# Turning q and k of the second batch over on DVE in 32x32 squares instead of on PE

## The chip, the cores and the metric

The kernel runs on one core of a Trainium2 chip. The metric is the device time of one execution in microseconds (us), lower is better. The engines are PE (TensorE: matmuls and transposes, results go to PSUM), DVE (VectorE), ACT (ScalarE), POOL (GpSimd) and SP (SyncE, here only a queue that issues DMAs). All data is float32 on the chip; the two weight matrices arrive as float64 and are narrowed on the chip.

## The reference

Attention that keeps the 32 largest scores of each row, and behind it a two-layer perceptron with an exact GELU:

```python
# q, k, v: (8, 8, 576, 64); w_in: (512, 2048); w_out: (2048, 512)
scores = q @ k.transpose(0, 1, 3, 2) / sqrt(64)
kth = np.partition(scores, -32, axis=-1)[..., -32:-31]
scores = np.where(scores >= kth, scores, -1e9)
attn = softmax(scores)                       # exp(s - max) / (sum + 1e-9)
x = (attn @ v).transpose(0, 2, 1, 3).reshape(8 * 576, 512)
h = x @ w_in
out = (0.5 * h * (1 + erf(h / sqrt(2)))) @ w_out
```

## The kernel before

**Tiles.** The 8 heads of a batch are taken as 4 pairs, so there are 32 pairs; pair 4 to 7 are the second batch. A pair's 576 rows are four tiles of 128 rows (two heads at a time) and a rest of 64; the rests of two pairs make one more item. A batch has 18 items, and the kernel 144.

**The main loop.** It runs over slots n = 0 to 147 and writes out, in program order, the work of several items at different stages: DVE looks for the 32 largest of item n (`top_k`: MAX8 and MATCH_REPLACE8), PE makes the scores of item n + 2 (`scores`, L370 and L385), ACT applies the softmax of item n - 1 (L495, L496), POOL divides it by its sum (`normalise`, L507), PE turns over the probabilities of item n - 2 (`transposes`, L527 and L553) and multiplies those of item n - 3 with v (`attend`, L615), and ACT copies that product into `xT` (L620). From slot 11 on PE's remaining time is filled with pieces of the perceptron (`mlp`: L673 for the first layer, L755 and others for the second); before that, with dummy matmuls (`keep_busy`, L995). Each engine works its instructions off in this order. A slot closes on DVE with the reciprocal of the softmax's sums (`inverse`, L482), which waits for POOL's `den` (L488), which waits for ACT's exponentials.

**Keys and queries.** Scores need q and k with the head dimension on the partitions, so both are turned over, pair by pair, into `kt` (keys, and the rest rows of q) and `qm` (q). A pair has three pieces: c = 0 (four key tiles), c = 1 (the rests of k and q), c = 2 (four query tiles). There are two ways. `by_pe` (L281) has PE transpose the 128x128 tiles of `raw_k` and `raw_q` into a PSUM bank, `tp_qk`, from which ACT copies them (L286). `squares` (L268, L270, L272) has DVE transpose 32x32 blocks straight from `raw_k` and `raw_q` into `kt` and `qm`; for that `load` brings the data in with the blocks' places already exchanged, in 16 transfers a pair (L109), with rows of 128 bytes, instead of 8 transfers (L116, L119) with rows of 256 bytes. `SQUARES` is the first pair that goes by DVE. A pair below it has one of two raw buffers, by its parity (the second lies in an unused part of `w_sum`), and its loads are issued when the pair two before it has been read; a pair from `SQUARES` on has the one buffer, and its loads are issued when the pair just before it has been read.

**Where the pieces stand.** `slots_of` gives the slots of the pieces by PE, `squares_of` those by DVE, both counted from the first item of the batch (18 for the second batch). Pieces by DVE stand at the head of their slot, behind `larger` (L406); pieces by PE stand among the transposes of the slot.

**PSUM.** `bank` hands out four banks in turn up to slot 12 and from slot 13 on the one bank "z" (`few`), which `tp_qk`, `tp_t` and `o` share.

**Weights.** `w_in` and `w_out` come in 16 units of two 128x512 parts. `load_weights` (L188, on SP) is called at the end of the slot two before the one in which the unit is added up; ACT (L205, L206, L212) or DVE (L208) splits the words in the slot before, and POOL adds them (L227).

Of the kernel before, what the change touches and what calls it, by code (L numbers as in the profile page):

```python
# [14 lines left out]
def kernel(  # L15
# [30 lines left out]
    NP = H // 2  # L46
# [38 lines left out]


    n_pairs = B * NP
    SQUARES = 2 * NP
    sources = {"q": q, "k": k, "v": v}

    def raw_of(n, pair):
        if n != "v":
            return raws[n][pair % 2 if pair < SQUARES else 0]
        return raws[n][pair % len(raws[n])]

    def load(n, pair, queue=None, queue2=None):
        if pair >= n_pairs:
            return
        queue = queue or nc.sync
        queue2 = queue2 or queue  # L100
        b, h0 = pair // NP, 2 * (pair % NP)
        src = sources[n]
        if n != "v" and pair >= SQUARES:
            t = flat[n][0]
            for e in range(2):
                for d in range(2):
                    rows, cols = slice((2 * e + d) * SQ, (2 * e + d + 1) * SQ), slice(d * SQ, (d + 1) * SQ)
                    for at, lo, hi, by in ((0, 0, SM, queue), (SM + e * TL, SM, S, queue2)):
                        by.dma_start(  # L109
                            out=t[rows, at : at + hi - lo].rearrange("i (c j) -> i c j", j=SQ),  # L110
                            in_=src[b, h0 + e, lo:hi, cols].rearrange("(c i) j -> i c j", i=SQ),
                        )
            return
        t = raw_of(n, pair)
        for e in range(2):
            queue.dma_start(  # L116
                out=t[:, 0:NM, e, :], in_=src[b, h0 + e, 0:SM].rearrange("(t p) d -> p t d", p=P)
            )
            queue2.dma_start(out=t[e * TL : (e + 1) * TL, NM, e, :], in_=src[b, h0 + e, SM:S])  # L119
# [140 lines left out]
    def transpose_qk(pair, first=False):  # L260

        q_tail = SM + P
        done = set()

        def squares(c):
            rq, rk, kt = flat["q"][0], flat["k"][0], kt_of.get(pair)
            if c == 0:
                nc.vector.transpose(kt[:, 0:q_tail], rk)  # L268
            elif c == 1:
                nc.vector.transpose(kt[:, q_tail:], rq[:, SM:])  # L270
            else:
                nc.vector.transpose(q_of[pair], rq[:, 0:SM])  # L272

        def by_pe(c):
            rq, rk = raw_of("q", pair), raw_of("k", pair)
            group = (
                [(rk, j) for j in range(NM)], [(rk, NM), (rq, NM)], [(rq, j) for j in range(NM)]
            )[c]
            tp = bank("tp_qk")
            for x, (r, j) in enumerate(group):  # L280
                nc.tensor.transpose(  # L281
                    tp[:, x * P : (x + 1) * P], r[:, j].rearrange("p e d -> p (e d)"), ident
                )
            dst = (kt_of[pair][:, 0:SM], kt_of[pair][:, SM:], q_of.get(pair))[c]
            copy = nc.vector.tensor_copy if first and c < 2 else nc.scalar.copy
            copy(out=dst, in_=tp[:, 0 : len(group) * P])  # L286

        def piece(c):
            if c == 0:
                kt_of[pair] = work.tile([P, 2 * P + SM], f32, tag="kt", bufs=NP + 2, name="kt")  # L290
            if c == 2:
                q_of[pair] = work.tile([P, SM], f32, tag="qm", bufs=NP, name="qm")
            (squares if pair >= SQUARES else by_pe)(c)
            done.add(c)
            ahead = 1 if pair >= SQUARES else 2
            if pair + ahead > SQUARES and pair < SQUARES and pair % 2:
                return
            if c != 0 and done >= {1, 2}:
                load("q", pair + ahead)
            if (c == 0 if pair >= SQUARES else c != 0 and done >= {0, 1, 2}):  # L300
                load("k", pair + ahead)

        return [lambda c=c: piece(c) for c in range(3)]
# [694 lines left out]
    for pair in range(2):  # L998
# [12 lines left out]
    squares_of = [  # L1011
# [4 lines left out]
    ]  # L1016
    first = {2: (0, 1, 1), 3: (2, 2, 3)}
    prep_in, squares_in = {}, {}
    for pair in range(2, n_pairs):
        b, p = divmod(pair, NP)  # L1020
        if pair >= SQUARES:
            trio = transpose_qk(pair)
            for at, c in squares_of[b % 2 * NP + p]:
                squares_in.setdefault(starts[b] + at, []).append(trio[c])
            continue
        for at, piece in zip(first.get(pair, slots_of[b % 2][p]), transpose_qk(pair)):
            prep_in.setdefault(starts[b] + at, []).append(lambda _, piece=piece: piece())
# [140 lines left out]
```

## Time and profile before

| | |
|---|---|
| runs | 1553.4, 1556.66, 1557.61 us; median 1556.66 |
| profiled execution | 1557.3 us, its span 1555.5 us, granted PE clock 0.994 |
| busy in the span | PE 98%, DVE 86%, ACT 75%, POOL 73% |
| DMA | 56.35 MB in 185298 packets, 176161 of them under 512 bytes |

The span runs from the first to the last instruction of the program; the execution's own time has 1.8 us more around it. An engine's busy time is the time in which at least one of its instructions runs; matmuls overlap, and their ends are modelled. In a group of instructions the last column is the time that the engine stood idle just ahead of them, with the instruction of another engine that ended it. A name as `L281` is a line of the kernel, and a `q` behind an engine's name its queue.

### The profile page before, as it was taken

How to read it: one execution, taken by the hardware profiler on the slowest of the kernel's cores; microseconds unless marked ns; L12 is line 12 of the kernel's file. 1: busy time of each engine (PE TensorE's matmuls, PEld its weight loads, DVE VectorE, ACT ScalarE, POOL GpSimd, SP SyncE). 2: the span in 40 equal slices, each digit the busy share in tenths (PEclk: the TensorE clock that was granted, in tenths of full speed). 3: DMA queues.
4: the chain of work that ended last, by engine and by line, in shares of the span. 5: the costliest groups of instructions: out<-in, count | busy, mean ns of one | idle time of the engine just before them, and what ended most of it. 6: DMA issues, size and time to landing. Idle time of an engine off the chain costs nothing. (4 is left out here: it accounts for less than half of the span.)

```text
span 1555.5 us, 28139 instructions
## 1 busy us (share of the span) xinstructions
PE 1522.8 (98%) x9280; PEld 1199.5 (77%) x9280; DVE 1330.3 (86%) x4571; ACT 1165.3 (75%) x2050; POOL 1141.5 (73%) x1291
## 2 busy tenths in 40 slices
PE   7899999999999999999999999999999999999998
PEld 5676578877777778887777778787877777787887
DVE  8998799989999988998989997988998998988700
ACT  6998877767777777777777778777777777777720
POOL 4886567767787868777787877776788786877632
PEclk9999999999999999999999999999999999999999
DMA  6513210012101111012201111002110111000000
GB/s 180 158 61 117 89 45 1 1 37 54 24 15 31 35 26 31 1 30 42 39 18 16 30 31 45 1 23 36 34 24 22 24 30 32 15 1 15 7 14 14
DMA packets 185298, 56.35 MB, mean 36 GB/s; under 512 B 176161, under 2 KB 176705, under 8 KB 185153
## 3 DMA queue, kind: packets, MB, share of 16 engines
q1 hardware_dynamic: 183888, 54.13, 14.6%
q8 instruction: 73, 1.20, 0.3%
q14 instruction: 73, 0.59, 0.1%
q10 hardware_dynamic: 1200, 0.39, 0.1%
q0 software_dynamic: 64, 0.03, 0.0%
HBM read 45.08 MB, written 9.44 MB: 35 GB/s over the span
## 5 line engine op out<-in xcount | busy, mean ns | idle before, releaser
L673 PE MATMUL h_ps<-xT,w_in_sb 128*128 128x256 f32 (+1 forms) x2560 | 541.4, 362 | 1.9 <-ACT xT L620 1.9
L673 PEld LDWEIGHTS h_ps<-xT,w_in_sb 128*128 128x128 f32 x2560 | 435.4, 191 | 73.4 <-issue 25.3
L450 DVE MAX8 top<-lists 128x8 f32<-128x288 f32 x792 | 321.1, 447 | 0.0
L507 POOL TENSOR_TENSOR s<-s,rden 128x1152 f32<-128x1152 f32 x144 | 302.7, 2102 | 0.3 <-DVE rden L482 0.3
L496 ACT ACTIVATE s<-s,bias 128x576 f32<-128x576 f32 x288 | 223.3, 775 | 11.9
L453 DVE MATCH_REPLACE8 lists<-top,lists 128x288 f32<-128x288 f32 x528 | 229.8, 443 | 0.0
L495 ACT ACTIVATE s<-s,neg 128x576 f32<-128x576 f32 x288 | 225.7, 784 | 2.8 <-POOL neg L475 2.7
L450 DVE MAX8 low<-lists 128x8 f32<-128x288 f32 x528 | 213.1, 445 | 0.0
L574 ACT COPY pt<-tp 128x1024 f32<-128x1024 f32 x133 | 134.8, 1014 | 96.1 <-PE tp L553 96.1
L488 POOL TENSOR_SCALAR den<-den 128x2 f32<-128x2 f32 x144 | 31.4, 218 | 236.0 <-ACT s L496 232.1
L421 POOL TENSOR_TENSOR lists<-lists 128x576 int32<-128x576 int32 x132 | 186.3, 1411 | 4.0
L413 POOL TENSOR_TENSOR lists<-s 128x576 int32<-128x576 int32 x132 | 185.6, 1406 | 0.0
L553 PE MATMUL tp<-ident,s 128*128 128x128 f32 x1152 | 150.7, 274 | 7.7 <-POOL s L507 7.7
L553 PEld LDWEIGHTS tp<-ident,s 128*128 128x128 f32 x1152 | 133.7, 141 | 27.3 <-POOL s L507 14.0
L615 PE MATMUL o<-pt,raw_v 128*64 128x256 f32 x1280 | 154.1, 386 | 0.4 <-ACT pt L560 0.4
L615 PEld LDWEIGHTS o<-pt,raw_v 128*64 128x64 f32 x1280 | 86.9, 137 | 87.0 <-issue 44.7
L475 POOL TENSOR_SCALAR neg<-kth 128x2 f32<-128x2 f32 x132 | 85.6, 649 | 88.3 <-DVE kth L466 88.3
L482 DVE RECIPROCAL rden<-den 128x2 f32<-128x2 f32 x144 | 23.4, 162 | 139.8 <-POOL den L488 138.6
L811 PE MATMUL y_ps<-w_out_sb,sum 128*128 128x256 f32 x480 | 142.8, 379 | 0.0
L378 ACT ACTIVATE s<-s_ps 128x1024 f32<-128x1024 f32 x127 | 124.3, 1025 | 15.7 <-PE s_ps L370 15.5
L370 PE MATMUL s_ps<-kt,qm 64*128 64x512 f32 x512 | 131.2, 626 | 0.8 <-ACT s L376 0.8
L453 DVE MATCH_REPLACE8 lists<-low,lists 128x288 f32<-128x288 f32 x264 | 114.9, 443 | 0.0
(148 smaller groups left out, 2784.1 us busy)
## 6 DMA issues: line engine op xcount, KB each, us to landing
raw_v<-in_v_dram SPq DMA_DIRECT2D x64, 128.0 KB, 2.4
out_dram<-y SPq DMA_DIRECT2D x30, 256.0 KB, 2.1
w_out_sb<-in_moe_w_in_dram SPq DMA_DIRECT2D x14, 511.8 KB, 4.9
raw_q<-in_q_dram SPq DMA_DIRECT2D x96, 64.0 KB, 2.0
raw_k<-in_k_dram SPq DMA_DIRECT2D x96, 64.0 KB, 2.0
w_out_sb<-in_moe_w_out_dram SPq DMA_DIRECT2D x10, 511.8 KB, 4.1
w_sum<-in_moe_w_out_dram SPq DMA_DIRECT2D x6, 511.8 KB, 4.1
raw_q<-in_q_dram SPq DMA_DIRECT2D x96, 8.0 KB, 1.8
```

The source lines that it names most:

```text
L413: nc.gpsimd.tensor_tensor(t[:, 1].bitcast(i32), a.bitcast(i32), b.bitcast(i32), op=ALU.add)
L421: nc.gpsimd.tensor_tensor(both, both, top, op=ALU.subtract)
L450: nc.vector.max(x[:, e], src[:, e])
L453: nc.vector.match_replace(dst[:, e], x[:, e], src[:, e], LOWEST)
L495: nc.scalar.activation(s, s, func=AF.Prelu, bias=st["neg"][:, e : e + 1], scale=1.0, alpha=STEEP)
L496: nc.scalar.activation(s, s, func=AF.Exp, bias=st["bias"][:, e : e + 1], scale=1.0, accum_out=st["den"][:, e : e + 1],)
L507: nc.gpsimd.tensor_tensor(s, s, wide, op=ALU.mult)
L553: nc.tensor.transpose(tp[:, j * P : (j + 1) * P], s[:, first + j * P : first + (j + 1) * P], ident)
L574: nc.scalar.copy(out=pt_now[0][:, 0 : 2 * NM, x : x + P], in_=tp.rearrange("p e (j n) -> p (e j) n", j=NM),)
L615: nc.tensor.matmul(o[e * D : (e + 1) * D, 0:n], lhsT=vt[:, j, e, :], rhs=pt[:, e * NM + j if j < NM else 2 * NM, :], start=(j == 0), stop= ...
L673: nc.tensor.matmul(h_tile(u)[:, i, :], lhsT=w_in_sb[:, ko, f * P : (f + 1) * P], rhs=xT[:, ko, c0 : c0 + n], start=(ko == 0), stop=(ko == ...
L811: nc.tensor.matmul(acc[names][:, k], lhsT=lhsT, rhs=rhs, start=(j == 0 and k == 0), stop=(j == FT // 2 - 1 and k == 1),)
```

## The change

`SQUARES` falls from 8 to 4, so that pairs 4 to 7 go by DVE too. A list of its own, `second`, gives their pieces' slots: 12 to 17. Pairs 0 to 3 stay with PE.

```diff
-    SQUARES = 2 * NP
+    SQUARES = NP
...
+    second = [
+        [(-6, 0), (-5, 1), (-5, 2)], [(-5, 0), (-4, 1), (-4, 2)],
+        [(-3, 0), (-3, 1), (-3, 2)], [(-2, 0), (-2, 1), (-1, 2)],
+    ]
...
         if pair >= SQUARES:
             trio = transpose_qk(pair)
-            for at, c in squares_of[b % 2 * NP + p]:
+            for at, c in second[p] if b == 1 else squares_of[b % 2 * NP + p]:
                 squares_in.setdefault(starts[b] + at, []).append(trio[c])
             continue
```

The pieces of pairs 4 to 7 stood in slots 8 to 10, 11 to 13, 14 and 15, and 15 and 16. In the new program the 40 transposes L281 and 12 copies L286 of these pairs are gone, twelve DVE transposes stand in slots 12 to 17, and the loads of pairs 4 to 7 are 64 transfers instead of 32: pair 4's are issued in slot 1, where they stood before, pair 5's in slots 12 and 13, pair 6's in 13 and 14, pair 7's in 15. The order of all else on PE, ACT, DVE and POOL is as before.

## The prediction

> **What bounds the kernel now.** A *slot* is one pass of the kernel's main loop; I cut the trace where DVE's reciprocal (L482) starts, which happens once in a slot. Read first is the page's list of engines: it names PE, but as an average over stages.
>
> ```profile
> PE 1522.8 (98%) x9280; PEld 1199.5 (77%) x9280; DVE 1330.3 (86%) x4571; ACT 1165.3 (75%) x2050; POOL 1141.5 (73%) x1291
> ```
>
> The stage is therefore read by itself, in the view of stretches: slots 11 to 17, from one reciprocal to the next. A row gives stretch, length, busy time and count of PE, PEld, DVE, ACT, POOL, then PE's granted clock, DMA share and GB/s.
>
> ```profile
> 112.33:123.90 11.57, 11.33 (x55) 8.13 (x53) 8.85 (x32) 7.43 (x15) 5.87 (x6) 0.90 0.48 127
> 123.90:133.29 9.39, 9.18 (x55) 7.30 (x56) 8.86 (x33) 9.25 (x17) 5.87 (x6) 1.00 0.34 132
> 133.29:145.98 12.69, 12.46 (x51) 5.99 (x49) 9.45 (x34) 12.52 (x20) 8.62 (x7) 1.00 0.08 18
> 145.98:157.43 11.45, 10.77 (x75) 8.30 (x71) 9.46 (x34) 8.74 (x16) 8.62 (x7) 1.00 0.64 213
> 157.43:169.65 12.22, 11.47 (x55) 5.78 (x53) 9.45 (x33) 12.05 (x18) 8.62 (x7) 1.00 0.09 16
> 169.65:182.07 12.42, 11.96 (x80) 8.38 (x79) 9.46 (x34) 9.12 (x16) 8.62 (x7) 1.00 0.46 121
> 182.07:194.08 12.01, 12.01 (x54) 5.79 (x54) 8.78 (x32) 11.44 (x17) 5.38 (x5) 1.00 0.25 89
> ```
>
> PE fills nearly all of each row, ACT fills every second one, and DVE has 2.6 to 3.3 us over in all but slot 12. The groups of this stretch (busy us and mean ns, then idle time before and its releaser) say who waits for whom.
>
> ```profile
> L553 PE MATMUL tp<-ident,s 128*128 128x128 f32 x56 | 7.4, 273 | 0.0
> ...
> L281 PE MATMUL tp_qk<-ident,w_sum 128*128 128x128 f32 x20 | 3.3, 281 | 1.4 <-ACT qm L286 0.7 <-ACT kt L286 0.5 <-ACT pt L537 0.2
> L281 PE MATMUL tp_qk<-ident,raw_q 128*128 128x128 f32 x9 | 2.0, 345 | 0.0
> L281 PE MATMUL tp_qk<-ident,raw_k 128*128 128x128 f32 x5 | 0.9, 284 | 0.7 <-ACT kt L286 0.7
> ...
> L482 DVE RECIPROCAL rden<-den 128x2 f32<-128x2 f32 x7 | 1.2, 166 | 14.6 <-POOL den L488 14.6
> ```
>
> DVE idles 14.6 us for `den`, the end of a chain that PE and ACT carry. PE never waits for the rows that DVE and POOL prepare (L553, 0.0). So here the order of PE's work sets the pace, and a matmul taken out of it is worth its place in the queue.
>
> **The change part by part.**
>
> *PE's transposes go.* Those of pairs 4 to 7 stand in slots 8 to 16; 34 of the 40 lie in the stretch above (the three L281 groups: 20 + 9 + 5). Their busy time is no price, since matmuls overlap; the distance from one start to the next is.
>
> ```profile
> 119.35 0.60 PE L281 MATMUL tp_qk<-ident,w_sum 128*128 128x128 f32 x4
> 119.79 0.27 PE L527 MATMUL tp_t<-ident,s 128*128 128x128 f32 x1
> ```
>
> Four starts in 0.44 us are 0.11 us each: 34 x 0.11 = 3.7 us. Then there are the waits between them. All share one PSUM bank from slot 13 on, so a second piece in a slot waits until ACT has copied out the first:
>
> ```profile
> 154.29 0.60 PE L281 MATMUL tp_qk<-ident,raw_k 128*128 128x128 f32 x4
> 155.57 0.33 PE L281 MATMUL tp_qk<-ident,raw_k 128*128 128x128 f32 x1 [0.68 <-ACT kt L286]
> ```
>
> The groups give 1.4 + 0.7 = 2.1 us of such idle time. It is counted from the modelled end of a matmul: the fifth could have started at 154.29 + 4 x 0.11 = 154.73 and started at 155.57, so 0.84 was lost where 0.68 is shown. With 0.16 more on each of four waits the transposes cost 3.7 + 2.1 + 0.6 = 6.4 us of PE's order. The first four of slot 11 ran at half pace (that row's clock is 0.90); I don't count this as gain, because the matmuls behind them inherit the slow stretch. Bounds: 3.7 us if all the waits turn up at another place, 7 us if something of the slow pace is won too. I take 6.4, because the order of PE's other instructions is unchanged in the built program and their next use of that bank comes at least one score matmul later.
>
> *ACT's copies go.* In slots 8 and 9 PE is filled with dummy matmuls, and ACT is what runs without a gap up to the first matmul of the second layer that waits for it:
>
> ```profile
> 94.20 0.61 ACT L286 COPY kt<-tp_qk 128x512 f32<-128x512 f32 x1
> 94.68 1.28 ACT L205 ACTIVATE w_out_sb<-w_out_sb,high 128x1024 f32<-128x1024 int16 x1
> ```
>
> ```profile
> 103.56 0.39 ACT L286 COPY kt<-tp_qk 128x256 f32<-128x256 f32 x1
> 103.83 1.29 ACT L205 ACTIVATE w_out_sb<-w_out_sb,high 128x1024 f32<-128x1024 int16 x1
> ```
>
> ```profile
> 110.47 0.70 PE L673 MATMUL h_ps<-xT,w_in_sb 128*128 128x256 f32 x2 [1.86 <-ACT xT L620]
> ```
>
> From start to start the two copies take 0.48 and 0.27 us, so `xT` comes 0.75 us earlier (bounds 0 and 0.75). The later copies lie beside PE's transposes and are not counted again.
>
> *DVE's squares come.* Their price stands in the groups of DVE over the whole run, where pairs 8 to 31 have them already:
>
> ```profile
> L268 DVE STREAM_TRANSPOSE kt<-raw_k 128x640 f32<-128x640 f32 x24 | 20.1, 838 | 0.0
> ...
> L272 DVE STREAM_TRANSPOSE qm<-raw_q 128x512 f32<-128x512 f32 x24 | 16.3, 678 | 0.0
> ...
> L270 DVE STREAM_TRANSPOSE kt<-raw_q 128x128 f32<-128x128 f32 x24 | 7.1, 298 | 0.2 <-issue 0.2
> ```
>
> That is 0.84 + 0.68 + 0.30 = 1.8 us a pair, 7.3 us in all, over slots 12 to 17. Per slot: slot 12 gets 0.84, which makes DVE 8.86 + 0.84 = 9.7 where the slot had 9.39; slots 13 and 15 get 1.8 each (11.3 of 12.69 and 12.22); slot 14 gets 1.0 (10.5 of 11.45); slot 16 gets 1.1 (10.6 of 12.42); slot 17 gets 0.7 (9.5 of 12.01). Only slot 12 runs over, by 0.3 us, and slot 13 has more than that to spare. Cost: nothing, with DVE's idle time for `den` as cover; without it, up to the 0.3 of slot 12. What waits for the squares comes late: the first scores of pair 4 and 5 are emitted in slot 16, of 6 and 7 in slot 17.
>
> *DMA.* A pair's k and q come in 16 transfers of 32x32 squares instead of 8. Two places matter, both on SP's queue, which issues in order. First the turn-round: k and q now have one buffer, so pair 7's loads start only when DVE has read pair 6 at the head of slot 15, and are read at the head of slot 16.
>
> ```profile
> 167.07 5.38 SPq L109 DMA_DIRECT2D raw_q<-in_q_dram  x8
> 172.49 3.96 SPq L109 DMA_DIRECT2D raw_k<-in_k_dram  x8
> 176.56 0.85 SPq L188 DMA_DIRECT2D w_sum<-in_moe_w_out_dram  x2
> ```
>
> Sixteen issues took 9.5 us there, with one hiccup; with some 2 us to land that is as long as a slot of 11 to 12 us. DVE may wait some tenths in slot 16, where it has 1.8 us over: cost nothing. Second, the start: pair 4's loads are issued in slot 1, and behind them on SP stands the weight load of slot 3.
>
> ```profile
> 26.34 0.37 SPq L116 DMA_DIRECT2D raw_q<-in_q_dram  x1
> ```
>
> ```profile
> 30.87 1.06 SPq L188 DMA_DIRECT2D w_sum<-in_moe_w_in_dram  x2
> ```
>
> ```profile
> w_sum<-in_moe_w_in_dram SPq DMA_DIRECT2D x2, 511.8 KB, 4.6
> ```
>
> ```profile
> 38.33 1.28 ACT L205 ACTIVATE w_sum<-w_sum,high 128x1024 f32<-128x1024 int16 x1
> ```
>
> ```profile
> 371.08 3.86 SPq L109 DMA_DIRECT2D raw_k<-in_k_dram  x8
> ```
>
> Now the two halves are issued by 31.9, the second lands about 4.6 us after its issue, at 36.3, and ACT reads them at 38.33: 2 us to spare. Eight square transfers take 3.9 us without a hiccup, sixteen 7.8: the weights are issued at 34.2 instead of 30.87, 3.3 us later, or 5 with the hiccup of 167.07. ACT then waits 1.3 to 3 us. I take 1.5, as the batch at 371.08 is the nearer in kind (no weights in flight). Nothing absorbs it: ACT is the engine without gaps from there on,
>
> ```profile
> 57.20:93.50 36.30, 36.30 (x293) 30.30 (x291) 34.79 (x125) 35.71 (x59) 32.82 (x28) 1.00 0.30 105
> ```
>
> (35.71 of 36.30; PE's figure holds the dummies), so `xT` at 110.47 comes 1.5 us later for it.
>
> *Sum.* -6.4 - 0.75 + 1.5 = -5.7 us. Behind slot 17 the program is the same, and the shift stays. The profiled execution took 1557.3 us (its span 1555.5 and 1.8 around it), so 1551.6; it lies 0.6 above the median of the runs shown, 1556.66, from which I get 1551.0.
>
> **The rivals.** *ACT carries the chain* (chance 0.2). ACT has 12.52 of 12.69 us in slot 13 and 12.05 of 12.22 in slot 15. If PE, once shorter, runs into ACT there, slots 12 to 17 yield only what ACT loses: 0.27 + 0.48 in slots 12 and 13 and some 1.2 in 14 to 16, by the copies above, instead of PE's 5. With 0.9 of slot 11 that is 2.9 instead of 6.4: 1556.66 - 2.9 - 0.75 + 1.5 = 1554.5. Against it: in slots 14 and 16 ACT is busy only 8.74 and 9.12 us and catches up.
>
> *The square transfers are slow, and the result is a slower kernel* (0.1). Place: SP's queue in slot 1. Where weights were landing, four 256-byte-row loads took 17.10 - 13.16 = 3.9 us to issue, 1.0 each:
>
> ```profile
> 13.16 0.59 SPq L116 DMA_DIRECT2D raw_k<-in_k_dram  x1
> ```
>
> ```profile
> 17.10 0.49 SPq L116 DMA_DIRECT2D w_sum<-in_q_dram  x1
> ```
>
> At that pace sixteen take 16 us, slot 3's weights are issued 11 us late and ACT waits 9 to 10 us; pair 7's q, by the same pace, comes 16 + 2 us after the head of slot 15, 4 us beyond what DVE has over. Together 9.5 + 4 - 7.1 = +6.4: 1563. It decides from 0.9 us an issue on, where ACT's wait alone eats the 7.1. Against it: the batch at 371.08 needs 0.48 an issue. [...]
>
> *PE's slow stretch goes too* (0.12). PE idles 1.86 us ahead of 110.47, and the clock granted in the next stretch is 0.90, so about 0.1 x 11.57 = 1.2 us is lost. If `xT`, coming earlier against PE's other work, leaves too short a gap, this is won: 1549.8. [...]
>
> That the change doesn't do what it says is excluded: in the built program L281 and L286 are gone from slots 8 to 16 and twelve L268/L270/L272 stand in slots 12 to 17.
>
> **How the numbers follow.** The forecast has 0.58, centre 1551.0; its own bounds are 1556.66 - 7 - 0.75 + 1.3 = 1550.2 and 1556.66 - 3.7 + 3 = 1556. The range is 1548 to 1557: from the clock rival with the best of the other terms, 1550.2 - 1.2 = 1549.0, to the forecast's upper bound, 1556, with 1 us on either side for the scatter of the runs shown (1553.4 to 1557.61); ACT's case lies within. No change means within 0.3%, 4.7 us, about what a measurement can tell, so 1552.0 is the line to "faster". Of the forecast about 0.43 lies beyond it (all but a hiccup in slot 1 or waits that come back), 0.15 within; the clock rival is faster, ACT's case is the same, the slow transfers give 0.08 slower and 0.02 the same. Faster 0.43 + 0.12 = 0.55, same 0.15 + 0.2 + 0.02 = 0.37, slower 0.08.
>
> **What would show it.** Right: slots 11 to 17 shorter by 6 to 7 us together, DVE's idle time for `den` there down from 14.6 to some 2 us, PE without a wait at ACT's copies, and an ACT wait of 1 to 3 us for `w_sum` near 38 us. Wrong: DVE waiting for raw_q or raw_k in slots 13 to 17; new PE idle time on `pt`, `xT` or `g` where L281 stood; slots behind 18 longer than before; or ACT's early wait near zero or above 5 us.

## The result, and the profile after

| | before | after |
|---|---|---|
| runs | 7 runs, 1553.03 to 1558.11 us; median 1554.42 | 7 runs, 1547.88 to 1551.39 us; median 1550.53 |
| ratio of the runs | | 0.9963, interval 0.9951 to 0.9975 |
| profiled execution | 1557.3 us, span 1555.5 | 1547.9 us, span 1546.1 |

By the ratio the kernel is faster by 0.37% (0.25 to 0.49%), some 5.8 us of 1554; the two medians of the table lie 3.9 us apart. In the experiments' runs the kernel before had medians of 1555.73 to 1556.23 us, so medians of different comparisons differ by 1 to 2 us without any edit; the steps below are therefore read in the traces.

The page's list of engines, of the changed kernel: PE has 40 transposes less, DVE 12 more, ACT 12 copies less.

```profile
PE 1513.3 (98%) x9240; PEld 1193.3 (77%) x9240; DVE 1336.4 (86%) x4583; ACT 1160.4 (75%) x2038; POOL 1142.8 (74%) x1291
```

The same view of stretches, slots 11 to 17 of the changed kernel (length; then busy time of PE, PEld, DVE, ACT, POOL; PE's granted clock; DMA share and GB/s):

```profile
112.56:121.58 9.02, 8.78 (x44) 5.95 (x42) 8.85 (x32) 6.36 (x13) 5.89 (x6) 1.00 0.01 3
121.58:131.11 9.53, 9.32 (x55) 7.41 (x55) 9.49 (x33) 9.39 (x18) 5.87 (x6) 1.00 0.44 105
131.11:142.92 11.81, 11.81 (x49) 5.63 (x49) 11.03 (x38) 11.64 (x17) 8.62 (x7) 1.00 0.39 79
142.92:153.12 10.20, 10.20 (x69) 7.67 (x69) 10.17 (x36) 8.14 (x14) 8.62 (x7) 1.00 0.64 182
153.12:164.55 11.43, 11.43 (x57) 5.36 (x51) 11.02 (x37) 11.26 (x17) 8.62 (x7) 1.00 0.44 100
164.55:174.88 10.33, 10.33 (x73) 7.59 (x69) 10.29 (x36) 8.36 (x14) 8.63 (x7) 1.00 0.48 132
174.88:186.18 11.30, 11.30 (x51) 5.52 (x45) 9.43 (x34) 11.03 (x17) 5.39 (x5) 1.00 0.43 119
sum 73.62, PE 73.17 PEld 45.14 DVE 70.28 ACT 66.17 POOL 51.65; mean PE 10.45 PEld 6.45 DVE 10.04 ACT 9.45 POOL 7.38
```

The seven slots last 73.62 us instead of 81.75, 8.13 less. From slot 13 on PE shows no gap at all (its busy time is modelled, as said), but DVE has now only 3.3 us over instead of 17. The groups of the same stretch:

```profile
L553 PE MATMUL tp<-ident,s 128*128 128x128 f32 x56 | 7.4, 273 | 0.0
...
L268 DVE STREAM_TRANSPOSE kt<-raw_k 128x640 f32<-128x640 f32 x4 | 3.3, 830 | 0.0
L272 DVE STREAM_TRANSPOSE qm<-raw_q 128x512 f32<-128x512 f32 x4 | 2.7, 679 | 0.0
L270 DVE STREAM_TRANSPOSE kt<-raw_q 128x128 f32<-128x128 f32 x4 | 1.2, 288 | 0.0
L482 DVE RECIPROCAL rden<-den 128x2 f32<-128x2 f32 x7 | 1.1, 162 | 1.5 <-POOL den L488 1.4
```

The L281 groups and their waits for `kt` and `qm` are gone, DVE's idle time for `den` has fallen from 14.6 to 1.4 us, and none of the squares waited for its data (0.0 in all three rows). Then the start, on SP's queue and on ACT:

```profile
26.39 3.87 SPq L109 DMA_DIRECT2D raw_q<-in_q_dram  x8
30.30 3.96 SPq L109 DMA_DIRECT2D raw_k<-in_k_dram  x8
34.31 0.90 SPq L188 DMA_DIRECT2D w_sum<-in_moe_w_in_dram  x2
```

```profile
40.09 1.27 ACT L205 ACTIVATE w_sum<-w_sum,high 128x1024 f32<-128x1024 int16 x1 [1.59 <-DMA w_sum<-in_moe_w_in_dram]
```

Sixteen issues took 7.9 us, the weights followed at 34.31 instead of 30.87, and ACT waited 1.59 us for them.

How the shift builds up is seen from the start of DVE's reciprocal at the end of each slot. The table gives that time minus the same one of the kernel before, in us, for the changed kernel and the experiments told below, each from its one profiled execution (the last column: end of the span):

| | 2 | 3 | 8 | 9 | 10 | 11 | 13 | 15 | 17 | 21 | end |
|---|---|---|---|---|---|---|---|---|---|---|---|
| after | +0.1 | +1.35 | +0.99 | +0.53 | +0.23 | -2.32 | -3.06 | -5.10 | -7.90 | -7.90 | -9.42 |
| PE's work back | +0.4 | +1.16 | +1.15 | +0.68 | +0.38 | -1.29 | -2.04 | -3.20 | -3.94 | -3.68 | -5.42 |
| ACT's work back | +0.7 | +1.09 | +1.44 | +1.49 | +1.52 | +0.65 | +0.73 | -0.78 | -3.59 | -3.59 | -5.26 |
| both back | +0.8 | +0.82 | +1.15 | +1.14 | +1.16 | +1.17 | +1.16 | +1.16 | +1.16 | +1.16 | +1.85 |
| DVE twice | +0.2 | +1.60 | +1.33 | +0.86 | +0.57 | -1.98 | -0.70 | -0.07 | -2.75 | -3.07 | -2.92 |
| one copy | +0.7 | +0.93 | +1.41 | +0.93 | +0.92 | +0.04 | -0.71 | -2.74 | -5.56 | -5.56 | -5.51 |
| weights first | +0.8 | +0.81 | -1.02 | -1.50 | -1.81 | -4.36 | -5.12 | -7.14 | -9.96 | -9.96 | -11.44 |

Of the changed kernel's 9.4 us, two pieces are no work taken away. In the kernel before, PE's clock was halved for some 3.4 us at the head of slot 11, and once more in its last products; the changed kernel's profile shows full clock in both places. Before (both stretches), then after (the same products):

```profile
110.50:114.50 4.00, 4.00 (x15) 3.43 (x16) 3.41 (x13) 2.59 (x6) 2.75 (x5) 0.58 0.00 0
1544.50:1548.00 3.50, 3.50 (x11) 2.77 (x10) 0.00 (x0) 0.73 (x2) 0.92 (x2) 0.53 0.00 0
```

```profile
110.75:114.75 4.00, 4.00 (x20) 2.84 (x20) 3.72 (x13) 2.85 (x7) 3.06 (x5) 1.00 0.00 0
1537.00:1540.50 3.50, 3.50 (x18) 3.09 (x17) 0.00 (x0) 0.74 (x2) 0.82 (x2) 1.00 0.00 0
```

In the last row 18 products start where 11 did before. That the end of the span lies 1.8 us further ahead than slot 144 (-9.42 against -7.60) is this second stretch.

### The profile page after: what moved, and what is told of

It reads as the page before. It is cut to its first block, busy times and chain, and to the rows that moved or that the text cites. A ratio compares the mean times of both kernels' runs of the same rounds, so it can differ in the third digit from the quotient of the medians.

```text
span 1546.1 us, 28114 instructions
## 1 busy us (share of the span) xinstructions
PE 1513.3 (98%) x9240; PEld 1193.3 (77%) x9240; DVE 1336.4 (86%) x4583; ACT 1160.4 (75%) x2038; POOL 1142.8 (74%) x1291
```

## The experiments

The theory is the prediction's: the gain is PE's order (transposes and their waits), paid for by one early wait of ACT; DVE's work is free. The rivals: ACT's copies were what counted; DVE's or the DMAs' new work costs something that hides in the sum; the clock made the difference.

**Both back.** Beside DVE's squares, the old transposes and copies are done again in their old slots, as dummies from `ident` into an unused buffer.

```diff
+    def old_way(c):
+        n = (4, 2, 4)[c]
+        tp = bank("tp_qk")
+        for x in range(n):
+            nc.tensor.transpose(tp[:, x * P : (x + 1) * P], ident, ident)
+        nc.scalar.copy(out=flat["k"][1][:, 0 : n * P], in_=tp[:, 0 : n * P])
```

> The changed kernel, with the PE transposes and the ACT copies of their results both put back as dummies at their old places: the old work beside the new. Theory: everything that the change took from PE and ACT comes back, 3.7 + 0.75 us and the waits in the shared bank, 2.1 to 2.7 us: the reciprocal of slot 20 comes 6 to 8 us later than in the changed kernel's trace, and the waits before the second piece of a slot (0.5 to 0.7 us each as the trace shows them) are there again. Rival (the waits would have been filled by DVE's or POOL's lateness): 4 to 5 us.

1558.67 us, ratio 1.0009 (0.9998 to 1.0021). Slots 11 to 17 of the kernel before, and of this one:

```profile
112.33:194.08 81.75, 79.18 (x413) 49.66 (x413) 64.31 (x228) 70.54 (x113) 51.58 (x45) 0.99 0.33 100
```

```profile
113.50:195.25 81.75, 79.19 (x412) 49.64 (x412) 70.34 (x241) 70.52 (x113) 51.61 (x45) 0.98 0.37 94
```

DVE is busy for 6 us more and the DMA traffic is the new one, and the seven slots last the same 81.75 us. The table's row is flat at +1.16 from slot 10 on. So beside the old order the squares and the later square transfers cost nothing; what this run is late by lies ahead of slot 8. The waits that the prediction read in the kernel before are back too (L1026 are the dummy transposes, L1027 their copies):

```profile
L1026 PE MATMUL tp_qk<-ident 128*128 128x128 f32 x34 | 6.1, 298 | 2.1 <-ACT w_sum L1027 1.9 <-ACT pt L537 0.2
```

At slot 21 this run is 9.06 us behind the changed kernel, where 6 to 8 were expected; 1.66 of them are a stretch of low clock, priced by the run *one copy* below.

**PE's work back alone, and ACT's alone.** The same dummies without the copies, and 12 copies within SBUF without the transposes.

```diff
+        tp = bank("tp_qk")
+        for x in range(n):
+            nc.tensor.transpose(tp[:, x * P : (x + 1) * P], ident, ident)
```

> The changed kernel, with the 40 PE transposes put back at their old places as dummies: they turn the identity over into the same PSUM banks, and nobody copies the result. Theory (each transpose is worth its place in PE's order, and the waits came from ACT's copies): the reciprocal of slot 20 comes 34 x 0.11 = 3.7 us later than in the changed kernel's trace, between 3 and 4.2, and no wait stands between the dummies. Rival (ACT's copies were what cost): under 1 us later.

```diff
+        nc.scalar.copy(out=flat["k"][1][:, 0 : n * P], in_=flat["q"][1][:, 0 : n * P])
```

> The changed kernel, with ACT's twelve copies put back at their old places as dummies, from SBUF to SBUF in an unused stretch, without PE's transposes. Theory (PE carries the chain from slot 11 on): only the two copies of slots 8 and 9 cost, 0.5 to 0.8 us, and of the later ones little, so the reciprocal of slot 20 comes 0.5 to 1.5 us later than in the changed kernel's trace. Rival (ACT carries the chain): 3 to 5 us later.

PE's back: 1552.31 us, ratio 0.998 (0.997 to 0.9989). ACT's back: 1552.03 us, ratio 0.9976 (0.9965 to 0.9987). Their slots 11 to 17, PE's first:

```profile
112.71:190.14 77.43, 76.81 (x407) 48.18 (x407) 70.33 (x240) 66.01 (x103) 51.59 (x45) 1.00 0.41 99
```

```profile
113.86:190.49 76.63, 75.79 (x385) 46.83 (x385) 70.28 (x240) 70.39 (x114) 51.65 (x45) 0.99 0.40 100
```

The transposes alone bring back 77.43 - 73.62 = 3.8 us. The copies alone bring back 3.0; but the clock stretch is back with them (the row's 0.99, from 112.5 to 116), and the run *one copy* below prices it at 1.66. That leaves 1.35 for ACT's copies there, where the theory wanted little. By the table 0.82 of it falls in slots 12 and 13 and 0.53 in slots 14 and 15. At slot 21 the run is 4.3 us behind the changed kernel, outside the theory's 0.5 to 1.5 and inside the rival's 3 to 5; without the clock it is 2.65, between the two. Both together take 8.13, or 6.5 without the clock: 3.8 of bare transposes, 1.3 of bare copies, and 1.3 that arises only where both are there. The 1.9 us that PE is shown to wait for copies with both back (0.2 for all with the transposes alone) cost less than their length.

**The last two pairs only.**

```diff
-    SQUARES = NP
+    SQUARES = NP + 2
```

> The change for pairs 6 and 7 alone; pairs 4 and 5 stay with PE and ACT, and pair 4's loads are the eight of before. Theory (PE's order is what counts, and the waits for ACT's copies in the shared bank are the larger part): no wait of ACT for weights near 38 us, slots up to 13 as before the change, and in slots 14 to 17 the 20 transposes (20 x 0.11 = 2.2 us) and their three waits (2.4 us) go: the reciprocal of slot 20 comes 4.0 to 4.8 us earlier than before the change. Rival (ACT carries the chain): what ACT loses in slots 14 to 16, 1.2 to 2.4 us.

1551.27 us, ratio 0.9976 (0.9966 to 0.9986). Up to slot 13 its trace lies within 0.2 us of that of before, then:

```profile
112.20:189.52 77.32, 76.61 (x394) 47.83 (x392) 67.31 (x235) 68.05 (x108) 51.61 (x45) 0.98 0.38 105
```

4.43 us of the 6.5 come from pairs 6 and 7, in slots 14 to 17, without the early cost: the loads that stand ahead of slot 3's weights are pair 4's, which goes by PE here.

**DVE twice.** Every square of pairs 4 to 7 is done twice.

```diff
+            for _ in range(2 if pair < 2 * NP else 1):
```

> The changed kernel with each of the twelve DVE transposes of pairs 4 to 7 done twice, 6.3 to 7.3 us more on DVE in slots 12 to 17. The changed kernel's trace leaves DVE only 3 us of idle time in these slots. Theory (DVE's idle time hid the first squares and is nearly used up): the reciprocal of slot 17 comes 3 to 4.5 us later, DVE's waits for den in slots 12 to 16 are gone, and DVE sets the pace there. Rival (PE stays the bound, since it lags up to 3 us behind DVE's results): under 1.5 us later.

1553.61 us, ratio 0.9982 (0.9972 to 0.9991).

```profile
112.91:191.33 78.42, 74.04 (x380) 45.32 (x380) 77.64 (x253) 66.86 (x104) 51.64 (x45) 1.00 0.38 95
```

The slots last 4.8 us longer than the changed kernel's and DVE fills 77.64 of 78.42. It had 73.62 - 70.28 = 3.3 us over and got 7.4 more, so 4.0 was the least; the reciprocal of slot 17 comes 5.15 us later, over the 3 to 4.5 expected. The cover that makes the squares free is thus nearly used up.

**Weights first.** Slot 3's weights are issued at the end of slot 0, ahead of pair 4's sixteen loads.

```diff
+        if n == 0:
+            load_weights(3)
         for m in (n + 1, n + 2):
-            if m > 2 and waits(unit_in(m)) == (m == n + 1):
+            if m > 3 and waits(unit_in(m)) == (m == n + 1):
                 load_weights(m)
```

> The changed kernel with one move: slot 3's weight load is issued at the end of slot 0, ahead of pair 4's sixteen loads, instead of behind them. Theory (the changed kernel loses some 1.6 us because ACT waits for this weight load near 40 us, and nothing behind it takes this back): ACT's wait there is gone, the reciprocals of slots 3 to 8 come 1.0 to 1.4 us earlier than in the changed kernel's trace, and the reciprocal of slot 20 too: the median falls by about 1.2 us against the changed kernel. Rival (the wait is swallowed by DVE's and PE's own idle time in slots 4 to 10): reciprocal of slot 20 as in the changed kernel, within 0.3 us.

1546.39 us, ratio 0.9946 (0.9933 to 0.996): faster than the kernel before. Its interval overlaps the changed kernel's (0.9951 to 0.9975), so the step between these two is read in the traces. The weights are now issued at 22.52, and ACT reads them without a wait:

```profile
22.52 1.06 SPq L188 DMA_DIRECT2D w_sum<-in_moe_w_in_dram  x2
```

```profile
38.17 1.26 ACT L205 ACTIVATE w_sum<-w_sum,high 128x1024 f32<-128x1024 int16 x1
```

At slots 10 to 21 it lies 2.04 to 2.06 us ahead of the changed kernel, more than the 1.0 to 1.4 expected and than the 1 us that the wait still cost there at slot 8. At that slot it is also 1.02 us ahead of the kernel before, which has no such wait, so a part of the 2 us is not a cost of the change won back. The stretch of low clock around 50 us is shorter too (48 to 51.5 us, where the changed kernel has 46.5 to 53), behind a PE gap of 2.64 instead of 5.05 us; how the 2 us divide between the two was not separated.

**The clock.** The stretch at slot 11 follows PE's wait for `xT`. The gap is 1.86, 1.86, 1.88 and 2.05 us in the four traces with the stretch (before, last two pairs, both back, ACT's back) and 1.51, 1.71, 1.72 and 1.73 in four without it (PE's back, weights first, after, DVE twice). So the change may have won the stretch only because `xT` comes nearer to PE's last product. Two runs filled the gaps ahead of the first product of `xT` and of the last product `seven` with 14 and 20 dummy products, in the changed kernel and in the version with the weights first:

```diff
+            if u == 0 and i == 0 and ko == KO - 1:
+                dummies(14)
...
+        if u == NU - 2:
+            dummies(20)
```

> The changed kernel with dummy matmuls added in two places where PE stands idle: 14 ahead of the first first-layer matmul that waits for xT (slot 10), 20 ahead of the last seven. Theory (the runs of both kernels scatter by 3 to 5 us because after each of these two gaps PE's clock is granted at half for some 3.4 us in some executions and not in others): no stretch with a granted clock of 0.5 near 111 us and near the end in the trace, all timed runs within 1.5 us of each other, and a median at the low end of the changed kernel's runs, about 1.5 to 2 us below its median. Rival (the scatter has another cause): runs scatter over 3 us as before and the median is that of the changed kernel or, with 34 matmuls more, up to 1 us above it.

> Both edits on top of the change: slot 3's weight load first, and the dummy matmuls in the two gaps. Theory: the two gains add, so about 3 us below the changed kernel's median and 8 to 9 us below the kernel before, ratio about 0.9945. Rival (one of the two is hidden): as the better one of them alone, 1.2 to 2 us below the changed kernel.

1552.18 us, ratio 0.998 (0.9971 to 0.9989), and 1549.65, ratio 0.9965 (0.9952 to 0.9977): by their medians both are slower than without the dummies, against the expectation. The trace of the first shows the dummies in the way:

```profile
109.26 3.39 PE L685 MATMUL idle<-ident 128*128 128x128 f32 x28 [0.26 <-ACT s L378]
112.49 0.60 PE L675 MATMUL h_ps<-xT,w_in_sb 128*128 128x256 f32 x2
```

Each dummy stands as two records, so 28 of them ran, until 112.49, where `xT` came at 110.70 in the changed kernel: 1.8 us late. With 5 and 10 dummies they end in time:

> The kernel before, with PE's two idle gaps filled: 5 dummy products (10 matmul records, 1.1 us) ahead of the first product of the second layer's xT, where PE idled 1.86 us, and 10 (20 records, 2.2 us) ahead of the last product `seven`, where it idled 2.43 us. Their ends lie before the data that the next product waits for, so they take no time of the path. Theory A (the clock falls after a PE gap of about 1.8 us or more, and this took part in the result): no stretch of low clock at 111 to 115 us nor in the last products, slot 11 ends 1.7 us earlier, the median 1.7 to 3 us under the kernel before (1553 to 1555), and the runs lie closer together. Theory B (the stretches come and go by execution, whatever PE does): a stretch in one of the two places stays in the profile or the median is unchanged within 1 us.

> The changed kernel with the same dummy products in both gaps. Theory A: no stretch in either place; the changed kernel's profile had none at 111 us and none in its last products, so slots 11 to 17 stay within 0.3 us of it, and the median is at the lower of its runs, 1548 to 1549. Against the kernel before with the same dummies it then stands 6.0 to 6.5 us lower: what the change brings without the clock (6.4 + 1.1 of ACT's copies - 1.35 of the weights). Theory B: unchanged median, 1550.5, and the same scatter, 3.5 us.

> The changed kernel with slot 3's weights issued ahead of pair 4's squares and the same dummy products in both gaps (the first form of this had 28 and 40 matmul records instead of 10 and 20, which stood 1.8 us over the arrival of xT). Theory A: 2.1 us under the changed kernel with dummies, 1546 to 1547, and its scatter about 1 us. Theory B: as the version without dummies, 1546.4 with runs up to 1549.6.

| both gaps filled | without | with | ratio to before |
|---|---|---|---|
| the kernel before | 1555.95 | 1553.56 (10 runs, 1552.72 to 1554.14) | 0.9987 (0.9978 to 0.9996) |
| the changed kernel | 1550.53 | 1548.64 (1546.31 to 1549.11) | 0.9951 (0.9937 to 0.9965) |
| weights first | 1546.39 | 1545.50 (1545.47 to 1545.77) | 0.9934 (0.9921 to 0.9946) |

("Without" is the median of each kernel's own comparison.) By the medians each gains 0.9 to 2.4 us by doing more work, by the ratios 1.9 to 2.0 each, though the intervals with and without dummies overlap in all but the first. The best version's five runs lie within 0.3 us; the changed kernel's still scatter over 2.8. (One execution of the kernel before with dummies, the profiled one, took 8976 us for a reason unknown; it is left out of its row, and as the trace is of this execution, there is none of that kernel to compare.) In the best version the dummies stand in the gap and `xT` sets the time:

```profile
106.72 1.37 PE L685 MATMUL idle<-ident 128*128 128x128 f32 x10
108.58 0.70 PE L675 MATMUL h_ps<-xT,w_in_sb 128*128 128x256 f32 x2 [0.49 <-ACT xT L620]
```

With the gaps filled in both, the change brings 1553.56 - 1548.64 = 4.9 us by the medians, or 5.6 by the ratios (0.9987 - 0.9951 = 0.0036 of 1556), less than the 6.0 to 6.5 expected.

**One copy.** The reverse test: one ACT copy more in slot 9 of the changed kernel.

```diff
+    def one_copy(_):
+        nc.scalar.copy(out=flat["k"][1][:, 0 : 2 * P], in_=flat["q"][1][:, 0 : 2 * P])
```

> The changed kernel with one ACT copy of 128x256 more in slot 9, where the kernel before copied a transposed piece out (0.27 us from start to start there). xT comes 0.27 us later, and PE's gap ahead of it grows from 1.72 to some 1.98 us. Theory A: the stretch of low clock at about 111.5 to 115 us is back, and slots behind 11 lie 0.3 + 1.7 = 2.0 us behind the changed kernel's. Theory B, and every theory in which only ACT's path counts: 0.3 us.

1551.43 us, ratio 0.997 (0.9959 to 0.9981). The gap, the clock behind it, and slots 11 to 17:

```profile
111.39 0.70 PE L673 MATMUL h_ps<-xT,w_in_sb 128*128 128x256 f32 x2 [2.01 <-ACT xT L620]
```

```profile
111.90:115.90 4.00, 4.00 (x15) 3.27 (x13) 3.43 (x14) 2.10 (x6) 2.77 (x5) 0.59 0.00 0
...
113.25:188.53 75.28, 74.83 (x379) 46.31 (x378) 70.28 (x241) 66.10 (x104) 51.63 (x45) 0.98 0.40 102
```

and the changed kernel's gap:

```profile
110.70 0.70 PE L673 MATMUL h_ps<-xT,w_in_sb 128*128 128x256 f32 x2 [1.72 <-ACT xT L620]
```

The stretch is back, and the seven slots last 75.28 - 73.62 = 1.66 us longer with the same work in them. In this execution a copy of 0.27 us costs 2 us up to slot 11; the medians, 1551.43 and 1550.53, lie 0.9 apart. So the change's profile holds 1.66 us of clock at this place.

## Why the prediction was right

The forecast was 1551.0, the median is 1550.53. That the two lie within 0.5 us is in part luck. The forecast subtracts 5.65 from 1556.66, the median of the three runs shown, and the kernel before has 1554.42 over seven runs; and the changed kernel's runs fall in two groups, three of 1547.88 to 1548.58 at a granted clock of 0.996 and four of 1550.53 to 1551.39 at 0.994 or 0.995, with the median at the edge of the second. The profiled execution is one of the first group. The mechanism is therefore judged by its steps, in the traces:

- *PE's order, -6.4*: slots 11 to 17 fell by 8.13, 6.47 of it not clock. The bare transposes were put at 3.7 and measured 3.8. The waits with the copies were put at 2.7, and the copies beside the transposes are worth 2.7 (1.35 + 1.3). But 1.35 of that comes back with ACT's copies alone, where PE has no transpose to hold up: the prediction booked it as waits of PE and said that these copies need not be counted again. The sum came out, its split only in half. (Of the 2.1 us read off the groups, 0.2 were a wait for `pt`, not for a copy.) That the groups of idle time understate a wait, the 0.16 added to each, was not tested by itself. Slot 11 alone, by *one copy*'s row, gave 0.88 for the 0.9 named there.
- *ACT's copies in slots 8 and 9, -0.75*: +0.99 at slot 8, +0.53 at 9, +0.23 at 10: 0.46 and 0.30 for the 0.48 and 0.27.
- *ACT's early wait, +1.5*: the wait is 1.59, but only 1.0 of it was left at slot 8. The cover denied there ("nothing absorbs it") exists: +1.35 at slot 3 has become +0.97 by slot 5. At slot 8 the six rows of the table with the late weights stand at +0.99 to +1.44, and the trace of the last two pairs, without the wait, at -0.12. This term was too large by 0.1 to 0.5.
- *DVE's squares, 0, and the turn-round of the buffer, 0*: held beside the old order, by *both back* to 0.01 us over seven slots, and none of the squares waited for its data (the rows of L268, L270 and L272). In the changed kernel's own order, where DVE has 3.3 us over and not 17, that they cost nothing is argued from the sum and not tested. DVE's share per slot came out up to 0.3 us under the figures given; slot 14 had 2.0 us over before (11.45 - 9.46), not at least 2.6 as the prediction says of all but slot 12.
- *ACT carries the chain*: refuted as a sum, 6.47 came instead of 2.9, and PE's transposes alone brought back 3.8. In part it holds. In slots 13 and 15 ACT is at 11.64 of 11.81 and 11.26 of 11.43, close to its limit, and there ACT's copies alone cost 0.82 and 0.53 us (with slots 12 and 14), while the six transposes put back in slots 12 and 13 cost nothing there (-0.75 us with them, -0.74 without). In slots 14 to 17 the transposes put back cost 2.9 us, more than the 20 x 0.11 = 2.2 that stand there, so the cost of the six seems to show up behind. PE and ACT share the pace in these slots.
- *The square transfers are slow*: refuted. Beside the 0.49 us an issue above, they land in 2.0 us, over the whole run:

```profile
raw_q<-in_q_dram SPq DMA_DIRECT2D x112, 64.0 KB, 2.0
```

A queue slowed down to 0.9 us an issue, as the rival needed, did not come.

- *PE's slow stretch goes too* (given 0.12): in the profiled execution it did, by the route described. It was priced at 1.2 from the mean clock and measures 1.66. The gap ahead of `xT` was 1.72 us where it had been 1.86, a difference that a sum of terms of 0.1 us can hardly foresee. With three of seven runs at the profile's clock, a chance nearer to a half would have been right; where the other four lost their clock, no trace shows.

Without the clock the trace gives +1.0 - 0.76 - 6.47 = -6.2 for the -5.65 forecast; the ratio of the runs, some 5.8 below, and the comparison with filled gaps, 4.9 or 5.6 below, lie a little under it. Why the last is under the trace stays open, as one of its two kernels has no trace to compare.

## What to carry to other kernels

Price an instruction taken from the engine that has no gaps at its start-to-start distance plus the waits it drags along (here 0.11 us a transpose: 3.7 us reckoned for 34, 3.8 measured), and price what is given to another engine by that engine's idle time in the same slots, not over the span: here the squares (6.0 us more of DVE's busy time beside the old order) were free, and doing them twice (7.4 more) cost 4.8. Look at what each moved DMA passes on its issuing queue: putting one weight load ahead of sixteen small loads brought 2 us more. And where PE waits (here 1.86 and 2.43 us), look at the granted clock behind the wait before explaining a difference of 2 us; a few dummy products that end before the data comes (here 5 and 10) brought 0.9 to 2.4 us by the medians, and in the best version the runs with them lie within 0.3 us.

## What the hardware showed beyond expectation

In the kernel before, PE's clock was halved for 3.41 us behind an idle gap of 1.86 us (at `xT`), and again behind one of 2.43 us (ahead of the last `seven`). The first of these stretches:

```profile
111.12:114.53 3.41, 3.41 (x14) 2.94 (x13) 2.82 (x10) 1.99 (x5) 2.16 (x5) 0.50 0.00 0
```

At the wait for `xT` the nine traces without fillers are sorted by the gap's length: none of the four up to 1.73 us has the stretch, all five from 1.86 us on have it. In the kernel before it begins 0.65 us after the end of this gap (111.12 after 110.47) and 1.33 us after the end of the other (1544.72 after 1543.39). Length alone doesn't settle it: the gap of 2.43 us ahead of the last `seven` is the same in nine traces, and four of them (before, both back, DVE twice, one copy) have a stretch in the products behind it. What settles it there was not shown. As two versions of the changed kernel (DVE twice, one copy) have the stretch too, its absence from the changed kernel's profile is not shown to be work of the change.
